# An attention and gated-MLP kernel: tokens by batches of 576 instead of chunks of 512, and each weight piece loaded once

## The chip, the cores and the metric

One Trainium2 chip, one of its cores. The metric is device time in microseconds (us), the median of several executions. Beside them one execution was taken by the hardware profiler; all durations below come from that one.

## The reference

Two stages on the same tokens. Attention has 8 batches, 8 heads, 576 positions and 64 columns a head; its output is the sum of a coarse attention over means of four positions, repeated four times, and a local attention in which a position sees those less than four away. The 4608 tokens of 512 columns then go through a gated MLP whose three weights come as float64:

```python
def _moe_ref(x, w_gate, w_val, w_out):          # x 4608x512, gate and val 512x1536, out 1536x512
    gate = 1.0 / (1.0 + np.exp(-(x @ w_gate)))
    val = x @ w_val
    return (gate * val @ w_out).astype(np.float32)

def _attn_ref(q, k, v):                         # each 8x8x576x64
    ...
    out_up = np.repeat(out_d, factor, axis=2)   # attention on means of 4 positions
    ...
    out_local = np.matmul(attn, v)              # mask: abs(i - j) < 4
    return (out_up + out_local).astype(np.float32)
```

## The kernel before, in words

**Attention units.** Two heads of one batch make a unit, four units a batch, 32 in all (`unit_steps`). A unit sums four positions on GpSimd (`prep2`, `vdsum`), forms the local scores (`s`) and the coarse ones (`sd`) on TensorE, normalizes both on VectorE, ScalarE and GpSimd, transposes them (`at`, `adt`), multiplies with v (`x`, `od`), adds the two (`xs`), and writes 576 columns of the MLP's input `xT` as two float16 tiles, a high part and a low part. Units 0 to 7 (the first two batches) multiply in float32, later ones in float16 parts.

**Weights.** Each weight is 12 pieces of 128x512 float64 words, 512 KB each: `wg`, `wv` and `wo`, 36 pieces. All 36 are loaded twice. In the first pass (`wstep` with "m") VectorE takes the largest magnitude of a piece from its high words (`wmax`, L153, tile `hmx`). When the `wg` and `wv` pieces of a group (0 to 3, 4 to 11), or all of `wo`, have theirs, a maximum over all partitions gives their scale (`wscale`, `gscales`, `ratios`). In the second pass (`wstep` with "c", `wconv`) a piece is loaded again; ScalarE multiplies its high words by the scale `hc` (L206), VectorE makes a float32 of the two words by a shift (L207), an or (L208) and the merging of the sign bit (L209), and the float32 is split into two float16 parts: by ScalarE (L215) and GpSimd (L216) for `wg` and `wv`, by ScalarE (L157) and VectorE (L158) for `wo`.

**MLP.** Tokens go in nine chunks of 512, and the weights in twelve steps `fc` a chunk: `moe_gate` (12 matmuls of 512 columns into `pg`, then tanh on ScalarE, L622, in one to two segments, as a chunk can lie in two batches), `moe_val` (12 matmuls into `pv`; VectorE multiplies, L630; ScalarE and VectorE split the product into float16, L638 and L639), `moe_out` (12 matmuls, three into each of the four output banks `po`). A product of float16 pairs is three matmuls (`product`, L395). The four `po` banks stay open for a whole chunk, so `wo`'s pieces are wanted one by one.

**PSUM.** Six banks belong to the MLP (`pg`, `pv`, four `po`), two to attention (`ps_a`).

**Order.** A table `T` gives each step a position, `add` collects the steps, and they are issued in the order of their positions; a scheduler then orders the instructions of each engine. Up to position `c1` = 56 the first two batches of attention, the weights and chunk 0 are woven together; from there each step of three matmul blocks (gate, val, out of the step before) takes the attention steps due. `awake` fills TensorE's waits of the first batch with matmuls on zeros. All loads and stores go through SyncE's queue (SP), in order.

Of the kernel before, what the change touches and what calls it, by code (L numbers as in the profile page):

```python
# [9 lines left out]
F16 = mybir.dt.float16  # L10
# [9 lines left out]
T = dict(ma=4.5, mas=0.45, mb=9.5, mbs=0.5, c1=56, gs=2.66, g0=16.84, r1=1.99, rs=1.6, ob=3.16, v0=15.13, v1=16.62, v2=17.5, vs=2.12, o0=18, os=1.2, pro=2.36, u4=13.82, u5=21, u6=27, u7=32, l4=1.3, l5=2.77, l6=9.47, l7=8.68, lv=15.08, vm=1.58, b8=6.75, s8=6.63, b12=26.05, s12=8.17, hold=32.07, al=0.76, am=1, z=3.68, sd=0, sn=0.79, v0m=0.61, xd=[2, 3, 7], ad=[0, 3, 7], aa=[0, 1, 2, 3, 6], td=[0, 3, 9, 10], vd=[], a_prep1=-2.43, a_prep2=-0.89, a_s0=0.01, a_s1=0.52, a_sm=1.82, a_d0=2.39, a_d1=2.6, a_dn=5.17, a_a0=4.37, a_vd=2.6, a_a1=5.1, a_v=2.74, a_at=5.22, a_od=5.79, a_x=8.38, m_prep0=-3.14, m_prep1=-1.14, m_prep2=-1.43, m_s0=0.69, m_s1=2.59, m_sm=3.12, m_d0=2.84, m_d1=5.8, m_a0=10, m_dn=10.78, m_vd=11.67, m_a1=12, m_v=13.07, m_at=13.44, m_od=15.64, m_x=17, k0=30, k_prep1=4, k_prep2=0, k_s0=2, k_s1=2, k_sm=4, k_d0=3, k_d1=0, k_dn=0, k_a0=3, k_vd=8, k_a1=2, k_v=5, k_at=0, k_od=0, k_x=0)  # L20
# [6 lines left out]
R = 58  # L27
# [8 lines left out]
NCHUNK = NT // CH  # L36
NFC = DFF // P
# [7 lines left out]
NWT = 1 + 2 * NPC  # L45
NST = 5
# [3 lines left out]
WAHEAD = 1  # L50
MAHEAD = 3
WGROUPS = [(0, 4), (4, NPC)]
SIGNBIT = -(1 << 31)


# [3 lines left out]
def attention_moe(ctx, tc, qk, qkd, v, vd, wg, wv, wo, mask, out):  # L59
# [5 lines left out]
    ps_o = ctx.enter_context(tc.tile_pool(name="ps_o", bufs=1, space=PSUM))  # L65
    ps_a = ctx.enter_context(tc.tile_pool(name="ps_a", bufs=2, space=PSUM))

# [3 lines left out]
    def awake(n):  # L73
        pt = ps_o.tile([P, 512], F32, tag="val", name="awake")
        for i in range(n):
            nc.tensor.matmul(pt[:, :256], idle[:, :P], idle, start=True, stop=True)

    awake(T["k0"])
# [4 lines left out]
    wg16 = cp.tile([P, NFC, 2, 4, P], F16, tag="wg16", name="wg16")  # L83
    wv16 = cp.tile([P, NFC, 2, 4, P], F16, tag="wv16", name="wv16")
    wo16 = cp.tile([P, NFC, 2, DM], F16, tag="wo16", name="wo16")
# [7 lines left out]
    def borrow(i, n):  # L93
        taken[i] += n
        return room[i][:, NFC * WPC - taken[i] : NFC * WPC - taken[i] + n]

    def zeroed(eng, shape, dtype, name):
# [59 lines left out]

# [698 lines left out]
```

## Time and profile before

| | |
|---|---|
| runs | 1107.99, 1111.20, 1111.18 us; median 1111.18 |
| the profiled execution | 1110.07 us, of which the span from first to last instruction is 1108.3 us |
| mean granted TensorE clock | 0.973 |
| busy over the span | TensorE 96%, VectorE 49%, ScalarE 40%, GpSimd 33% |
| moved | 99.84 MB read, 9.44 MB written |

PE is TensorE, PEld its weight loads, DVE VectorE, ACT ScalarE, POOL GpSimd, SP SyncE. A busy TensorE is one that has a matmul in flight, which tells nothing of useful work: the fillers count, and a matmul at the lower clock counts longer. The profile's page also follows the chain of work that ended last, and lists groups of instructions with their mean time and with the idle time in front of them.

### The profile page before, as it was taken

The numbers are of one execution on the slowest core, as the hardware profiler recorded it, in microseconds if no ns is written. First come the engines' busy times: TensorE is split into PE (matmuls) and PEld (weight loads), VectorE is DVE, ScalarE is ACT, GpSimd is POOL, SyncE is SP. The second block draws the span as 40 slices with busy tenths as digits, with TensorE's granted clock in tenths as the row PEclk, the third lists the DMA queues.
The fourth block names the chain that finished last, engine by engine and source line by source line (L and its number), as shares of the span: only waits on it lengthen the run. The fifth ranks groups of instructions, "written<-read, shape, count | busy, mean of one in ns | idle before, by whom it ended". The sixth has DMA issues, their size and how long they took to land.

```text
span 1108.3 us, 17149 instructions
## 1 busy us (share of the span) xinstructions
PE 1062.2 (96%) x6831; PEld 554.8 (50%) x6831; DVE 547.4 (49%) x1038; ACT 444.1 (40%) x1048; POOL 364.6 (33%) x426
## 2 busy tenths in 40 slices
PE   8768878999998999999999999999999999999998
PEld 6543434655554555555555555555555544444443
DVE  5779989763445444444444444444444422212112
ACT  5535656443444443444334443444344422112112
POOL 8535755332433443333333443333332200000000
PEclk9859988999999999999999999999999999999999
DMA  9987866331213222232212221321120000000001
GB/s 361 382 313 262 275 211 210 110 118 59 70 56 136 70 71 70 71 109 71 70 57 101 74 80 59 109 71 59 59 97 1 2 1 38 1 1 38 1 1 38
DMA packets 31903, 110.38 MB, mean 100 GB/s; under 512 B 3536, under 2 KB 3664, under 8 KB 31824
## 3 DMA queue, kind: packets, MB, share of 16 engines
q1 hardware_dynamic: 31824, 109.30, 29.0%
q8 instruction: 54, 0.88, 0.3%
q14 instruction: 25, 0.20, 0.1%
HBM read 99.84 MB, written 9.44 MB: 99 GB/s over the span
## 4 chain that ended last, share of the span: by engine, by line
PE 86%; DVE 7%; POOL 2%; DMA 2%; ACT 2%; issue 1%; SPq 0%; DVEq 0%; POOLq 0%
PE po L395 25%; PE pv L395 24%; PE pg L395 23%; PE s L395 3%; PE x L395 3%; PE sd L395 3%; PE od L395 2%; PE at L543 2%; PE adt L553 1%; DMA qkd<-in_qkd_dram 1%; DVE hmx L153 1%; DVE wrv L209 1%; DVE wrg L208 1%; POOL kdblk L386 1%; DMA wg6c<-in_wg_dram 0%
## 5 line engine op out<-in xcount | busy, mean ns | idle before, releaser
L395 PE MATMUL pg<-xT,wg 128*128 128x512 f16 x1296 | 312.5, 383 | 11.2 <-ACT wg L215 7.3
L395 PE MATMUL pv<-xT,wv 128*128 128x512 f16 x1296 | 310.3, 381 | 5.3 <-DVE tanh L630 3.1
L395 PE MATMUL po<-g,wo 128*128 128x512 f16 x1188 | 281.2, 379 | 0.0
L395 PEld LDWEIGHTS <-wg 128*128 128x128 f16 x1296 | 125.3, 98 | 158.3 <-ACT wg L215 8.6
L395 PEld LDWEIGHTS <-wo 128*128 128x128 f16 x1296 | 126.4, 98 | 150.8 <-ACT wo L157 3.9
L395 PEld LDWEIGHTS <-wv 128*128 128x128 f16 x1296 | 125.6, 98 | 150.1 <-issue 6.4
L630 DVE SCALAR_TENSOR_TENSOR tanh<-tanh,pv 128x512 f32<-128x512 f32 x108 | 73.9, 684 | 210.2 <-PE pv L395 206.4
L622 ACT ACTIVATE tanh<-pg,tsc 128x512 f32<-128x512 f32 (+7 forms) x192 | 86.7, 497 | 176.4 <-PE pg L395 176.2
L638 ACT ACTIVATE g<-tanh,gs 128x512 f16<-128x512 f32 x99 | 71.4, 721 | 137.4 <-DVE tanh L630 135.6
L639 DVE SCALAR_TENSOR_TENSOR g<-tanh,gs,g 128x512 f16<-128x512 f32 x99 | 84.1, 849 | 52.9 <-ACT g L638 52.5
L477 POOL TENSOR_TENSOR t<-t,mx 128x640 f32<-128x640 f32 x32 | 43.4, 1357 | 164.0 <-DVE mx L476 160.1
L596 POOL TENSOR_TENSOR xT<-xs,xT 128x384 f16<-128x384 f32 (+7 forms) x54 | 48.5, 911 | 48.1 <-ACT xT L594 47.5
L585 DVE TENSOR_TENSOR xs<-x,od 128x464 f32<-128x464 f32 (+1 forms) x56 | 23.5, 452 | 72.3 <-PE x L395 72.3
L487 POOL TENSOR_TENSOR t<-t,sm 128x640 f32<-128x640 f32 x28 | 36.1, 1290 | 68.9 <-DVE sm L485 61.3
L465 DVE SCALAR_TENSOR_TENSOR t<-s,mk 128x384 f32<-128x384 f32 x64 | 30.8, 485 | 54.8 <-PE s L395 54.7
L157 ACT ACTIVATE vblk<-v,svb 64x640 f16<-64x640 f32 x48 | 39.6, 825 | 34.3 <-PE x L395 33.6
L395 PEld LDWEIGHTS s<-qk 64*64 64x64 f32 x1200 | 41.0, 138 | 21.5 <-issue 16.3
L158 DVE SCALAR_TENSOR_TENSOR vblk<-v,svb,vblk 64x640 f16<-64x640 f32 x48 | 47.9, 998 | 3.8 <-ACT vblk L157 1.7
L395 PE MATMUL s<-qk 64*64 64x64 f32 x1200 | 48.9, 227 | 0.6 <-ACT adt L535 0.6
L528 POOL TENSOR_TENSOR ad<-e,sme 72x288 f32<-72x288 f32 x52 | 37.1, 733 | 35.2 <-DVE sme L519 34.8
L511 ACT ACTIVATE e<-sd,mxd 72x144 f32<-72x144 f32 x128 | 47.1, 371 | 2.8
L384 POOL TENSOR_TENSOR qkd<-qkd 128x576 f32<-128x576 f32 x29 | 35.0, 1208 | 37.6 <-DMA qkd<-in_qkd_dram 36.9
(295 smaller groups left out, 1105.1 us busy)
## 6 DMA issues: line engine op xcount, KB each, us to landing
qk<-in_qk_dram SPq DMA_DIRECT2D x30, 610.0 KB, 3.9
qkd<-in_qkd_dram SPq DMA_DIRECT2D x29, 576.0 KB, 3.7
vd<-in_vd_dram SPq DMA_DIRECT2D x29, 384.0 KB, 3.1
v<-in_v_dram SPq DMA_DIRECT2D x32, 320.0 KB, 3.0
out_dram<-osb SPq DMA_DIRECT2D x16, 512.0 KB, 2.6
wo<-in_qk_dram SPq DMA_DIRECT2D x2, 610.0 KB, 9.9
wo<-in_qkd_dram SPq DMA_DIRECT2D x2, 576.0 KB, 9.5
out_dram<-osb SPq DMA_DIRECT2D x4, 256.0 KB, 2.4
```

The costliest lines, as they stand in the source:

```text
L157: nc.scalar.activation(hi, src, AF.Copy, scale=sc)
L158: nc.vector.scalar_tensor_tensor(out=lo, in0=src, scalar=sc, in1=hi, op0=ALU.mult, op1=ALU.subtract)
L395: nc.tensor.matmul(o, w[a], x[c], start=first and i == 0, stop=last and i == len(pairs) - 1)
L477: nc.gpsimd.tensor_tensor(out=t, in0=t, in1=mx.unsqueeze(2).to_broadcast([P, NBLK, WIN]), op=ALU.subtract)
L487: eng.tensor_tensor(out=t, in0=t, in1=sm.unsqueeze(2).to_broadcast([P, NBLK, WIN]), op=ALU.mult)
L511: nc.scalar.activation(s["e"][:, qb, h, :], pt[:QM, h * SD : (h + 1) * SD], AF.Exp, bias=mx[:, h : h + 1], scale=QKSCALE / 16, accum_out=s ...
L528: eng.tensor_tensor(out=AD[:, qb].rearrange("p c h k -> p h c k")[:, :, :, :KC], in0=s["e"][:, qb].rearrange("p h (c k) -> p h c k", c=NKC ...
L596: eng.tensor_tensor(out=x[:, hp, 1, o : o + n], in0=src, in1=x[:, hp, 0, o : o + n], op=ALU.subtract)
L622: nc.scalar.activation(t[:, o : o + n], pt[:, o : o + n], AF.Tanh, scale=tsc[:, b, fc : fc + 1])
L630: nc.vector.scalar_tensor_tensor(out=t, in0=t, scalar=1.0, in1=pt, op0=ALU.add, op1=ALU.mult)
L638: nc.scalar.activation(g[:, 0], t, AF.Copy, scale=gs[:, fc : fc + 1])
L639: nc.vector.scalar_tensor_tensor(out=g[:, 1], in0=t, scalar=gs[:, fc : fc + 1], in1=g[:, 0], op0=ALU.mult, op1=ALU.subtract)
```

## The change

- The MLP takes one batch of 576 tokens at a time, in two halves of 288 columns. A gate or val step is 24 matmuls of 288 columns in one PSUM tile of two banks (`mm`, two such tiles); tanh and the product take 576 columns in one instruction.
- `moe_out` does not run beside the gate and val steps any more. The float16 products of all twelve steps of a batch are kept (`gq`), and then four output blocks of 72 matmuls each run over all twelve `wo` pieces.
- Attention has four PSUM banks in place of two.
- A weight piece is loaded once. ScalarE multiplies its high words by a constant, VectorE makes the float32 at once (shift, or, sign) into the float16 home of the next piece, and its magnitude is taken from that float32 (`wjoin`). The scale comes later, for two pieces of `wg` and `wv` at a time (`wscale`), and is put on in `wsplit`: for `wg` and `wv` by one more VectorE instruction, for `wo` within the split. `wo` is scaled when all twelve magnitudes are known (`oscale`).
- Staging buffers are four in place of five, v buffers four in place of five; loads stand in one fixed order (`load`).
- The table `T` is new: it gives every step of the first four units its own position.

```diff
+HN = S // 2
-NST = 5
+NST = 4
-WGROUPS = [(0, 4), (4, NPC)]
+WGROUPS = [(0, 2), (2, 4), (4, 6), (6, 8), (8, 10), (10, NPC)]
-    ps_o = ctx.enter_context(tc.tile_pool(name="ps_o", bufs=1, space=PSUM))
-    ps_a = ctx.enter_context(tc.tile_pool(name="ps_a", bufs=2, space=PSUM))
+    ps_m = ctx.enter_context(tc.tile_pool(name="ps_m", bufs=2, space=PSUM))
+    ps_a = ctx.enter_context(tc.tile_pool(name="ps_a", bufs=4, space=PSUM))
+    def mm(name):
+        return ps_m.tile([P, 2, 512], F32, tag="mm", name=name)
...
-    def wmax(t, o):
-        absmax(o, t[:, :, 1].bitcast(F32))
...
-    def wconv(k, i, t, j):
+    def wjoin(k, i, after):
+        t = wraw.pop((k, i))
         h, l = t[:, :, 1], t[:, :, 0]
-        a = raw.tile([P, WPC], I32, tag="wa", name=f"wr{k}{i}", bufs=3)
-        nc.scalar.activation(h.bitcast(F32), h.bitcast(F32), AF.Copy, scale=hc[:, j : j + 1])
-        nc.vector.tensor_scalar(out=a, in0=h, scalar1=3, scalar2=None, op0=ALU.logical_shift_left)
+        a = wwide(k, i).bitcast(I32)
+        nc.scalar.activation(h.bitcast(F32), h.bitcast(F32), AF.Copy, scale=WORDS)
+        with behind(after):
+            nc.vector.tensor_scalar(out=a, in0=h, scalar1=3, scalar2=None, op0=ALU.logical_shift_left)
         nc.vector.scalar_tensor_tensor(out=a, in0=l, scalar=29, in1=a, op0=ALU.logical_shift_right, op1=ALU.bitwise_or)
         nc.vector.scalar_tensor_tensor(out=a, in0=h, scalar=SIGNBIT, in1=a, op0=ALU.bitwise_and, op1=ALU.bitwise_or)
+        absmax(hmx[:, j : j + 1], wwide(k, i))
...
+    def wsplit(k, i):
+        a = wwide(k, i)
+        hi, lo = (home[k][:, wslot(k, i), e] for e in range(2))
         if k == "o":
-            split(wo16[:, i, 0, :], wo16[:, i, 1, :], a.bitcast(F32), co[:, i : i + 1])
+            split(hi, lo, a, sc)
         else:
-            nc.scalar.copy(hi, src)
-            nc.gpsimd.tensor_tensor(out=lo, in0=src, in1=hi, op=ALU.subtract)
+            nc.vector.tensor_scalar(out=a, in0=a, scalar1=sc, scalar2=None, op0=ALU.mult)
+            nc.scalar.copy(hi, a)
+            nc.gpsimd.tensor_tensor(out=lo, in0=a, in1=hi, op=ALU.subtract)
...
+    def moe_in(b, w, x, k, fc, name):
+        pt = mm(name)
+        for h in range(2):
+            f = slice(h * HN, (h + 1) * HN)
+            for j in reversed(range(4)):
+                product(pt[:, h, :HN], [w[:, fc, a, j, :] for a in range(2)], [x[:, j, e, f] for e in range(2)], j == 3, j == 0)
+        return pt[:, :, :HN]
...
-    def moe_out(c, fc):
-        for e in range(4):
-            product(oacc[c][e], [wo16[:, fc, a, f] for a in range(2)], [g[:, a] for a in range(2)], fc == 0, fc == NFC - 1)
+    def moe_out(b, m):
+        assert all(("o", i) in done for i in range(NPC))
+        pt = mm(f"po_{b}_{m}")
+        for h in range(2):
+            for n in range(NFC):
+                fc = n // 2 + NFC // 2 * (n % 2)
+                product(pt[:, h, :HN], [wo16[:, wslot("o", fc), a, m * P : (m + 1) * P] for a in range(2)],
+                        [gq[:, fc, e, h * HN : (h + 1) * HN] for e in range(2)], n == 0, n == NFC - 1)
```

Where the instructions stand now, first on VectorE at the first weights of batch 0. Before, two conversions of the second pass (here `wg` and `wv` of step 8; `...c` is a piece loaded for conversion, `...m` one loaded for its maximum, `tanh` an MLP product):

```order
L207 TENSOR_SCALAR wrg_1362<-wg8c 128x512
L209 SCALAR_TENSOR_TENSOR wrv_1312<-wv7c,wrv_1312 128x512
L207 TENSOR_SCALAR wrv_1403<-wv8c 128x512
L208 SCALAR_TENSOR_TENSOR wrg_1362<-wg8c,wrg_1362 128x512
L153 TENSOR_REDUCE hmx<-wo11m 128x1
L630 SCALAR_TENSOR_TENSOR tanh_6_1564<-tanh_6_1564,pv_6_1595 128x512
L208 SCALAR_TENSOR_TENSOR wrv_1403<-wv8c,wrv_1403 128x512
L209 SCALAR_TENSOR_TENSOR wrg_1362<-wg8c,wrg_1362 128x512
```

And now, at the scaling of steps 2 and 3 and the first MLP product (L209 to L211 are the shift, the or and the sign, L160 the magnitude, L251 the scaling; `wg_109` and `wv_110` are the float16 homes):

```order
L160 TENSOR_REDUCE hmx<-wg_109 128x1
L160 TENSOR_REDUCE hmx<-wv_110 128x1
L251 TENSOR_SCALAR wg_109<-wg_109,cw 128x512
L251 TENSOR_SCALAR wv_110<-wv_110,cw 128x512
L251 TENSOR_SCALAR wg_109<-wg_109,cw 128x512
L251 TENSOR_SCALAR wv_110<-wv_110,cw 128x512
L209 TENSOR_SCALAR wg_109<-wg_927 128x512
L210 SCALAR_TENSOR_TENSOR wg_109<-wg_927,wg_109 128x512
L593 SCALAR_TENSOR_TENSOR tanh_0_852<-tanh_0_852,pv_0_876 128x576
```

The magnitude of a piece has stayed on VectorE and follows its own conversion; four scalings per two steps have come on top, in VectorE's queue ahead of the products.

Second, VectorE at the end of the weights. Before, the last three splits of `wo` (L158), with the MLP product of step 10 ahead of them and that of step 11 behind:

```order
L158 SCALAR_TENSOR_TENSOR wo_111<-wro_2062,co,wo_111 128x512
L583 SCALAR_TENSOR_TENSOR xs_2015<-x_8_2017,sxb,od_6_1959 128x112
L630 SCALAR_TENSOR_TENSOR tanh_10_1999<-tanh_10_1999,pv_10_2031 128x512
L209 SCALAR_TENSOR_TENSOR wro_2157<-wo11c,wro_2157 128x512
L639 SCALAR_TENSOR_TENSOR g_10_2045<-tanh_10_1999,gs,g_10_2045 128x512
L153 TENSOR_REDUCE vm_3148<-v_2991 128x1
L158 SCALAR_TENSOR_TENSOR wo_111<-wro_2111,co,wo_111 128x512
L158 SCALAR_TENSOR_TENSOR wo_111<-wro_2157,co,wo_111 128x512
L630 SCALAR_TENSOR_TENSOR tanh_11_2107<-tanh_11_2107,pv_11_2120 128x512
L639 SCALAR_TENSOR_TENSOR g_11_2134<-tanh_11_2107,gs,g_11_2134 128x512
```

And now, the last splits of `wo` (L165), between the attention of units 5 to 7 (`t`, `sm`, `xs`, `mxd`):

```order
L165 SCALAR_TENSOR_TENSOR wo_111<-wo_111,co 128x512 x2
L450 TENSOR_REDUCE sm_2281<-t_2160 128x10
L165 SCALAR_TENSOR_TENSOR wo_111<-wo_111,co 128x512
L550 SCALAR_TENSOR_TENSOR xs_2311<-x_0_2302,sxb,od_5_2279 128x464
L451 TENSOR_SCALAR sm_2281<-sm_2281 128x10
L165 SCALAR_TENSOR_TENSOR wo_111<-wo_111,co 128x512
L452 RECIPROCAL sm_2281<-sm_2281 128x10
L550 SCALAR_TENSOR_TENSOR xs_2311<-x_8_2313,sxb,od_5_2279 128x112
L165 SCALAR_TENSOR_TENSOR wo_111<-wo_111,co 128x512
L475 TENSOR_REDUCE mxd_1_2324<-sd_1_2322 72x2
```

All twelve splits of `wo` now come after the twelfth product of the first token block, where before they were spread among the products; 358 VectorE instructions stood up to the last split, and 382 stand there now.

Third, TensorE at the end of the first batch's output. `po_0` to `po_3` are the output blocks of the first 576 tokens, `x`, `od`, `adt`, `s` and `sd` attention of units 6 to 8, and `pg` and `pv` the next batch's first steps. Now:

```order
L367 MATMUL od_2593<-adt_7_2558,vdblk_117 128x144 x3
L367 MATMUL x_0_2601<-at_7_2435,vblk 128x58 x8
L367 MATMUL x_8_2612<-at_7_2435,vblk 128x58 x2
L367 LDWEIGHTS wo_111
L367 MATMUL po_3_2619<-gq,wo_111 128x288
```

Before, `wo` products of the first chunk began right behind the gate and val steps that fed them:

```order
L395 MATMUL s_3_1640<-qk_1143 64x64 x8
L395 MATMUL sd_0_1654<-kdblk_120,qks_1410 72x288
L395 LDWEIGHTS wo_111
L395 MATMUL po_0_1570<-wo_111 128x512
L395 LDWEIGHTS wo_111
L395 MATMUL po_0_1570<-wo_111 128x512
```

In the change the first two output blocks run side by side from behind unit 4's `x`, 35 matmuls of each ahead of the place where the last `wo` piece is wanted; behind it stand 37 of each, then 72 and 72 of the last two blocks.

## Rows read from the trace of the kernel before

**Rows 1.** The page's slices: the span in 40 slices of 27.7 us, busy tenths of TensorE and VectorE.

```profile
PE   8768878999998999999999999999999999999998
...
DVE  5779989763445444444444444444444422212112
```

**Rows 2.** Busy time by stretches of the span, first to second us: the length, then for each engine busy us and number of instructions, the granted clock (1.00 is 2.4 GHz, the lower level 0.50), DMA share, GB/s.

```profile
0.00:9.00 9.00, 7.87 (x77) 5.70 (x78) 2.31 (x6) 0.36 (x1) 5.44 (x12) 1.00 0.79 261
9.00:18.00 9.00, 6.65 (x69) 4.07 (x69) 7.66 (x16) 7.50 (x20) 8.54 (x13) 1.00 1.02 411
18.00:28.00 10.00, 9.91 (x93) 7.97 (x92) 6.57 (x16) 6.42 (x21) 8.49 (x13) 0.83 1.03 409
28.00:84.00 56.00, 39.89 (x241) 27.40 (x239) 44.39 (x100) 26.28 (x71) 22.26 (x28) 0.70 0.93 346
84.00:214.00 130.00, 111.62 (x627) 56.87 (x628) 123.85 (x224) 77.30 (x155) 74.40 (x62) 0.92 0.66 223
...
364.00:900.00 536.00, 536.00 (x3760) 282.45 (x3758) 247.28 (x475) 222.38 (x553) 193.27 (x237) 1.00 0.21 67
```

**Rows 3.** VectorE in order of time around 214 us: start us, duration us, engine, line, operation, out<-in, shapes, count, and in brackets the idle time before it with what ended it.

```profile
206.32 0.68 DVE L209 SCALAR_TENSOR_TENSOR wro<-wo10c,wro 128x512 int32<-128x512 int32 x1
...
212.60 1.40 DVE L158 SCALAR_TENSOR_TENSOR wo<-wro,co,wo 128x512 f16<-128x512 f32 x2
216.07 0.69 DVE L630 SCALAR_TENSOR_TENSOR tanh<-tanh,pv 128x512 f32<-128x512 f32 x1 [2.08 <-PE pv L395]
```

**Rows 4.** TensorE in order of time at the end of the span (columns as in rows 3); a row is a run of instructions of one kind.

```profile
1090.62 2.75 PE L395 MATMUL po<-g,wo 128*128 128x512 f16 x12
1093.20 2.75 PE L395 MATMUL pg<-xT,wg 128*128 128x512 f16 x12
1095.80 2.75 PE L395 MATMUL pv<-xT,wv 128*128 128x512 f16 x12
1098.38 5.34 PE L395 MATMUL po<-g,wo 128*128 128x512 f16 x24
```

**Rows 5.** TensorE from 640 to 672 us (columns as in rows 3): the run of short matmuls and the row behind it.

```profile
650.35 0.98 PE L395 MATMUL x<-at,vblk 128*128 128x58 f16 x30
651.17 0.81 PE L395 MATMUL po<-g,wo 128*128 128x512 f16 x3
```

**Rows 6.** Groups of TensorE instructions from 364 to 900 us: line, engine, operation, out<-in, shapes, count, busy us, mean ns of one, idle us before.

```profile
L395 PE MATMUL pg<-xT,wg 128*128 128x512 f16 x675 | 162.5, 379 | 0.0
L395 PE MATMUL pv<-xT,wv 128*128 128x512 f16 x672 | 161.6, 379 | 0.0
L395 PE MATMUL po<-g,wo 128*128 128x512 f16 x672 | 161.1, 379 | 0.0
L395 PE MATMUL s<-qk 64*64 64x64 f32 x720 | 28.7, 223 | 0.0
...
L395 PE MATMUL x<-at,vblk 128*128 128x58 f16 x600 | 20.0, 189 | 0.0
```

**Rows 7.** Groups of VectorE instructions over the span, shapes apart (columns as in rows 6, with the releasers of the idle time).

```profile
L639 DVE SCALAR_TENSOR_TENSOR g<-tanh,gs,g 128x512 f16<-128x512 f32 x99 | 84.1, 849 | 52.9 <-ACT g L638 52.5
L630 DVE SCALAR_TENSOR_TENSOR tanh<-tanh,pv 128x512 f32<-128x512 f32 x108 | 73.9, 684 | 210.2 <-PE pv L395 206.4 <-ACT t L478 1.9 <-ACT e L511 1.1
...
L508 DVE TENSOR_REDUCE mxd<-sd 72x2 f32<-72x288 f32 x64 | 28.6, 446 | 33.5 <-PE sd L395 33.4
...
L153 DVE TENSOR_REDUCE vm<-v 128x1 f32<-128x640 f32 x32 | 26.0, 815 | 35.4 <-DMA v<-in_v_dram 35.3
...
L518 DVE TENSOR_SCALAR sme<-sme 72x4 f32<-72x4 f32 x32 | 9.1, 285 | 20.7 <-ACT e L511 20.6
...
L487 DVE TENSOR_TENSOR t<-t,sm 128x640 f32<-128x640 f32 x4 | 3.6, 904 | 0.1
L158 DVE SCALAR_TENSOR_TENSOR xT<-xs,sxb,xT 128x512 f16<-128x512 f32 x4 | 3.4, 861 | 0.3 <-ACT xT L157 0.3
L583 DVE SCALAR_TENSOR_TENSOR xs<-x,sxb,od 128x464 f32<-128x464 f32 x4 | 2.8, 692 | 2.6 <-PE x L395 2.6
...
L158 DVE SCALAR_TENSOR_TENSOR xT<-xs,sxb,xT 128x64 f16<-128x64 f32 x4 | 1.4, 338 | 0.0
L583 DVE SCALAR_TENSOR_TENSOR xs<-x,sxb,od 128x112 f32<-128x112 f32 x4 | 1.3, 324 | 0.0
```

**Rows 8.** The conversion's three VectorE operations by stretch (L207 the shift, L208 the or, L209 the sign, in this order; of L207 both stretches): stretch, its length, VectorE busy us and count, clock, DMA share, GB/s.

```profile
18.00:84.00 66.00, 1.68 (x4) 0.72 0.95 356
84.00:214.00 130.00, 16.90 (x32) 0.92 0.66 223
...
84.00:214.00 130.00, 26.16 (x33) 0.92 0.66 223
...
84.00:214.00 130.00, 29.12 (x33) 0.92 0.66 223
```

**Rows 9.** VectorE from 126 to 140 us (columns as in rows 3): the sign merging of a `wg` piece.

```profile
133.21 1.46 DVE L209 SCALAR_TENSOR_TENSOR wrg<-wg7c,wrg 128x512 int32<-128x512 int32 x1
```

**Rows 10.** GpSimd in the same stretch.

```profile
132.97 1.15 POOL L216 TENSOR_TENSOR wv<-wrv,wv 128x512 f16<-128x512 f32 x1
```

**Rows 11.** Waits over the span: engine and line, what was waited for, us in total, times, the longest.

```profile
DVE tanh L630 <- PE pv L395: 206.4, 70, 5.5
...
DVE vm L153 <- DMA v<-in_v_dram: 35.3, 18, 5.6
```

## What the change does to the time, predicted

> **What bounds the kernel now.** I read the slices first, then the busy time by stretches, then the order of time on VectorE and TensorE at the border between them. The slices [rows 1] show two kernels in one: to about 210 us VectorE is at 7 to 9 tenths, from there TensorE stands at 9 to the end. The stretches [rows 2] sharpen it. From 84 to 214 us VectorE is busy 123.85 of 130 us; from 364 to 900 us TensorE is busy 536.00 of 536.00 and VectorE 247 of it. Before 28 us the DMA engines are full (share 1.02, 1.03), to 84 us nearly (0.93). The border is the last `wo` split [rows 3]: two splits end at 214.0 us, and the next product already waits 2.08 us for TensorE. So the span is **the time at which VectorE has finished the weights, plus TensorE's work that stands behind it**. Behind it come 1108.3 - 214.0 = 894.3 us. The last matmul ends at 1098.38 + 5.34 = 1103.7 us [rows 4], so 4.6 us of that are the last output's way out.
>
> Of the first 214 us VectorE is busy 2.31 + 7.66 + 6.57 + 44.39 + 123.85 = 184.8 and idle 29.2: 8.0 to 18 us, 15.0 from 18 to 84 us, 6.2 after [rows 2].
>
> **The change on VectorE.** The orders give 358 instructions up to the last split before and 382 now; by kind:
>
> - Shift, or, sign and the magnitude stay at 36 each: the second load goes, its VectorE work does not, for a magnitude was the first pass's only work there. Nothing.
> - 24 scalings of `wg` and `wv` (L251) are new: float32, 512 columns, in place. The nearest row is the shift, one input and a scalar: 16.90/32 = 0.53 us, and 1.68/4 = 0.42 in the quieter stretch [rows 8]. The other side is an instruction of 512 float32 columns with two inputs, one in PSUM, 0.684 [rows 7]. 24 x 0.53 = +12.7 (10.1 to 16.4), since the stretch is the crowded one.
> - MLP products: 12 pairs of 576 columns now stand before the last split, where 11 of 512 stood. A pair is 0.684 + 0.849 = 1.53 us [rows 7]; 12 x 1.53 x 1.125 - 11 x 1.53 = 20.7 - 16.9 = +3.8.
> - Two more normalizing products `t` at 0.904: +1.8. Five v magnitudes fewer at 0.815: -4.1. Part of unit 7 falls behind (`xs` 0.692 + 0.324, one `mxd` 0.446, one `sme` and its reciprocal, together some 0.45): -1.9. Four `xT` low parts in one piece of 576, between 0.861 and 0.861 + 0.338 each, say 0.97: -0.9 [all rows 7]. The small instructions on scales even out by count (some 45 against 47).
> - Crowding: in 84 to 214 us an or takes 26.16/33 = 0.79 and a sign merging 29.12/33 = 0.88 [rows 8], while an undisturbed one takes 0.68 [rows 3]; one of 1.46 us [rows 9] runs beside a GpSimd subtraction of 1.15 us [rows 10]. Now the joining comes earlier than the splits. If a third of the 33 x (0.11 + 0.20) = 10 us goes, that is -3 (0 to -10).
>
> Busy: 184.8 + 12.7 + 3.8 + 1.8 - 4.1 - 1.9 - 0.9 - 3 = 193.
>
> Idle: the 8.0 us at the start are the first unit's and stay; the 6.2 late ones I keep. The 15.0 from 18 to 84 us I put down mostly to loads: v magnitudes alone wait 35.3 us for them over the span [rows 11], and that stretch has the full DMA. Now 18.9 MB less come in and a loaded piece gives VectorE 2.4 us of work at once instead of a 0.67 us magnitude, so I keep 3 (0 to 15). Total idle 17. **The last split ends at 193 + 17 = 210 us**, 4 us earlier than now. The halved weight loading is thus worth little: it ran beside a VectorE that has as much to do.
>
> **The change on TensorE.** A matmul of 512 columns takes (1098.38 - 1090.62)/36 = 0.2156 us [rows 4]. One of 288 isn't in the trace in float16. Between (651.17 - 650.35)/30 = 0.0273 for 58 columns [rows 5] and 0.2156 for 512, a straight line gives 0.1227; pro rata without any fixed part it would be 0.1213. I take 0.1227: a weight load that took longer than 58 columns would show in that row. The MLP has 8 x 864 = 6912 matmuls now against 3888: 848 us against 838, +10, although the columns are the same.
>
> What can't start before the last `wo` piece is the point. Before, `wo` products ran as their pieces came, and 214 us found ten steps of the first chunk out. Now 35 matmuls of each of the first two output blocks stand ahead of the last piece, and 37 + 37 + 72 + 72 = 218 behind it: 218 x 0.1227 = 26.7 us. Then
>
> - what is left of units 6 and 7 in float32: some 7 us;
> - seven batches: 7 x 864 x 0.1227 = 742;
> - 24 units of attention. From 364 to 900 us 2019 MLP matmuls [rows 6] at 0.2156 take 435.3 of 536 us, and 100.7 remain; 600 `x` matmuls at 30 a unit are 20 units, 720 `s` at 40 are 18 (a few records are missing), 19.3 by what stands in that stretch, so 5.2 us a unit: 125 (120 to 134);
> - waits in the batches: +2. The gate and val tiles are two, so one must be emptied while the other fills. That was 2 x 2.59 us, now 24 x 0.1227 = 2.94, while product and tanh grow by an eighth;
> - the tail, 4.6.
>
> Together 907 us. **Span 210 + 907 = 1117, and with the 1.8 us that the profiled execution has around its span 1119 us**, against its own 1110.07 (the median of the runs shown, 1111.18, lies 1.1 above it). The 4 us of earlier weights are outweighed by 13 us more on TensorE: 218 + 6048 = 6266 matmuls take 769 us, where before (894.3 - 4.6 - 7 - 125)/0.2156 = some 3515 of 512 columns were left for 758; these are nearly the same columns (6266 x 288/512 = 3525), so +9 of it is the fixed part of a matmul, paid nearly twice as often.
>
> What is hidden: the float16 products kept for a batch, the four attention banks, tanh in one instruction and the new load order. From 227 us on TensorE covers all these; if it had idle time there, VectorE's 247 of 536 us still leave room.
>
> **Rivals.**
>
> 1. *Forecast* (0.44): VectorE keeps the border near 210 us, output stands behind.
> 2. *The joining gets much cheaper and the loads free VectorE* (0.29, ends faster). Against my 0.53 + 0.79 + 0.88 = 2.20 us for the three conversion steps stand the undisturbed 0.42 + 0.68 + 0.68 = 1.78 [rows 3, 8]. With splits later, half the pieces or more may be joined undisturbed, and the scalings too: 36 x 0.42 = 15 us and 24 x 0.11 = 2.6, of which -3 is already in; with idle time at 11, the early 8 and 3 more, the border is at about 191 us and the end near 1100. It decides from about 200 us down: there the gain covers the 13 us that TensorE gets on top. For it speaks the DMA share in the early stretch; against it that from 84 us VectorE is 95% busy with the DMA at 0.66, where loads can't be what it waits for.
> 3. *It cancels* (0.16): the border at 200 to 206 us, the end within 1108 to 1114.
> 4. *Two tiles for gate and val are too few* (0.10, slower). VectorE's product waits for TensorE 70 times now, up to 5.5 us [rows 11]: slack that the shorter block halves. If one in four of the 168 blocks of the last seven batches waits 0.6 us, that is +25: 1143.
> 5. *The weight loads come out from behind the matmuls* (0.01). From 364 to 900 us a load is 282.45/3758 = 0.075 us [rows 2], and 3024 more of them in the open would give +227: 1346. The row of 58 columns, a load and a matmul in 0.027 us, excludes it nearly.
>
> The Trainium skill, TensorE: Matmul & The Clock Gate, section Part 3, The mechanism, says that a weight load overlaps matmuls in flight only when the row groups differ; all these use the full array, and by that rule the fifth case would be the forecast. The trace disagrees: 36 pairs in 7.76 us leave 2.3 ns a pair beyond 512 columns at 2.4 GHz.
>
> **How the numbers follow.** About 0.3% (3.3 us) is what a measurement of this kernel can tell from no change, 1107.8 to 1114.5 us. Slower is the forecast, the fourth and fifth case, 0.55; same the third, 0.16; faster the second, 0.29. The forecast alone runs from 1112 (scalings at 0.42, crowding gone by half) to 1132 (0.684, no relief, six more us of idle). The range reaches down into the second case and up to the weaker half of the fourth: 1095 to 1140.
>
> **What the changed profile would show.** Right: the last `wo` split near 210 us with VectorE at 90% or more from 60 us on; 24 scalings of some 0.5 us; the first batch's output as a dense run on TensorE right behind, 27 us of matmuls; blocks of 24 in 2.94 us; no idle TensorE from 250 us; a lower DMA share before 84 us. Wrong: a last split below 200 us (second case), VectorE with long waits for DMA or scales before 150 us, TensorE waiting for `tanh` or `gq` in later batches (fourth), or a granted clock that falls while TensorE waits for `wo`, which would stretch the output at the lower level.

## The result, and the profile after

The changed kernel takes 1118.95 us (median of 5 runs, 1117.19 to 1122.24), the kernel before 1111.18. The ratio is 1.0078, 95% interval 1.0055 to 1.0101: slower by 0.8%. The forecast was 1119. The sum came out right; the event that it took for the border (the end of the last `wo` split) did not stand, and two of its terms were off by 3 and 5 us in opposite directions. The profiled execution took 1117.19 us, its span is 1115.4.

Busy tenths by slice, and busy time by the stretches of [rows 1, 2], now of the changed kernel:

```profile
PE   9695688999999999999999999999999999999998
...
DVE  7969999735552446314452346315452345302210
```

```profile
0.00:9.00 9.00, 7.95 (x73) 5.78 (x74) 2.79 (x7) 0.83 (x1) 6.93 (x15) 1.00 0.81 300
9.00:18.00 9.00, 9.00 (x100) 7.36 (x101) 7.30 (x21) 6.15 (x18) 7.05 (x12) 1.00 1.03 411
18.00:28.00 10.00, 9.93 (x114) 8.50 (x112) 9.83 (x17) 6.13 (x21) 8.04 (x10) 1.00 1.03 408
28.00:84.00 56.00, 44.06 (x298) 35.52 (x298) 45.80 (x99) 32.36 (x77) 19.48 (x17) 0.73 0.27 88
84.00:214.00 130.00, 99.19 (x835) 73.80 (x833) 126.20 (x244) 63.60 (x134) 62.77 (x56) 0.89 0.48 163
364.00:900.00 536.00, 536.00 (x5222) 430.97 (x5221) 231.54 (x446) 181.40 (x413) 171.09 (x204) 1.00 0.22 73
```

From 84 to 214 us VectorE is busy 126.20 of 130 us, as forecast, and TensorE less than before (99.19 against 111.62). From 28 to 84 us the DMA share has fallen from 0.93 to 0.27, yet VectorE idles 10.2 us there, against 11.6 before. From 18 to 84 us, the stretch of the prediction, it idles 10.4 us against 15.0.

TensorE in order of time, where the first batch's output begins and where the last `wo` split is wanted (in brackets the idle time and what ended it):

```profile
185.70 0.27 PE L135 MATMUL mxt<-ident,m1o 128*1 128x128 f32 x1 [2.79 <-DVE m1o L229]
...
194.80 2.58 PE L367 MATMUL po<-gq,wo 128*128 128x288 f16 x10 [1.78 <-ACT wo L164]
...
213.24 9.24 PE L367 MATMUL po<-gq,wo 128*128 128x288 f16 x74 [0.40 <-DVE wo L165]
222.32 0.90 PE L367 MATMUL od<-adt,vdblk 128*128 128x144 f32 x6
```

The last split ends at 213.2 us, and 74 output matmuls follow at (222.32 - 213.24)/74 = 0.1227 us each, the value taken in the prediction. But TensorE waits only 0.40 us there. Its last long waits are those at 185.7 us, for the maximum over the twelve magnitudes of `wo` (`m1o`), and at 194.8 us, for the first split. From there on output and attention fill it. The ten matmuls at 194.8 us took 2.58 us, where ten at 0.1227 take 1.23: the granted clock was 0.57 from 194 to 198 us, mostly the lower level of 1.2 GHz, behind the wait of 1.78 us. The prediction had named this as a sign of being wrong; it cost some 1.4 us.

The same view of the kernel before shows that there too the border was earlier than the prediction had it:

```profile
145.47 0.27 PE L126 MATMUL mxt<-ident,m1o 128*1 128x128 f32 x1
...
178.71 0.87 PE L395 MATMUL po<-wo 128*128 128x512 f16 x2 [2.83 <-ACT wo L157]
180.70 4.45 PE L395 MATMUL po<-wo 128*128 128x512 f16 x10 [1.12 <-DVE wo L158]
```

From 180.7 us on TensorE is without a wait until 345 us, though VectorE converts until 214: it had output products in hand. The first row is the maximum over the magnitudes of `wo`: it stood at 145.5 us, where it now stands at 185.7.

### The profile page after: what moved, and what is told of

Read it like the earlier page. It is cut to its first block, busy times and chain, and to the rows that moved or that the text cites. A ratio compares the mean times of both kernels' runs of the same rounds, so it can differ in the third digit from the quotient of the medians.

```text
span 1115.4 us, 23080 instructions
## 1 busy us (share of the span) xinstructions
PE 1067.4 (96%) x9935; PEld 853.8 (77%) x9935; DVE 544.6 (49%) x1046; ACT 393.6 (35%) x878; POOL 345.9 (31%) x395
## 4 chain that ended last, share of the span: by engine, by line
PE 84%; DVE 9%; ACT 2%; DMA 2%; POOL 1%; issue 1%; DVEq 0%; ACTq 0%; SPq 0%; POOLq 0%
PE po L367 25%; PE pg L367 22%; PE pv L367 22%; PE s L367 3%; PE x L367 3%; PE sd L367 2%; PE od L367 2%; PE at L510 1%; DVE hmx L160 1%; PE awake L83 1%; PE adt L520 1%; DMA wg<-in_wg_dram 1%; DVE wg L211 1%; DMA wo<-in_wo_dram 1%; DVE wv L210 1%
## 5 line engine op out<-in xcount | busy, mean ns | idle before, releaser
L367 PE MATMUL pg<-xT,wg 128*128 128x288 f16 x2304 | 307.2, 290 | 15.9 <-ACT wg L252 15.3
L367 PE MATMUL pv<-xT,wv 128*128 128x288 f16 x2304 | 302.0, 286 | 3.7 <-DVE tanh L593 3.5
L367 PE MATMUL po<-gq,wo 128*128 128x288 f16 x2304 | 289.9, 287 | 2.2 <-ACT wo L164 1.8
L367 PEld LDWEIGHTS <-wg 128*128 128x128 f16 x2304 | 225.2, 99 | 79.7 <-ACT wg L252 15.9
L367 PEld LDWEIGHTS <-wv 128*128 128x128 f16 x2304 | 224.2, 98 | 60.8 <-issue 4.1
L367 PEld LDWEIGHTS <-wo 128*128 128x128 f16 x2304 | 224.0, 98 | 59.9 <-ACT wo L164 2.1
L593 DVE SCALAR_TENSOR_TENSOR tanh<-tanh,pv 128x576 f32<-128x576 f32 x96 | 72.1, 751 | 200.4 <-PE pv L367 200.4
L164 ACT ACTIVATE gq<-tanh 128x576 f16<-128x576 f32 x96 | 65.6, 683 | 198.1 <-DVE tanh L593 197.4
L588 ACT ACTIVATE tanh<-pg,tsc 128x576 f32<-128x576 f32 x96 | 70.8, 738 | 125.6 <-PE pg L367 125.4
L165 DVE SCALAR_TENSOR_TENSOR gq<-tanh,gq 128x576 f16<-128x576 f32 x96 | 77.8, 810 | 23.8 <-ACT gq L164 22.9
L165 DVE SCALAR_TENSOR_TENSOR vblk<-v,svb,vblk 64x640 f16<-64x640 f32 x48 | 46.6, 971 | 5.1 <-ACT vblk L164 4.3
```

Source lines behind the costliest of these rows:

```text
L164: nc.scalar.activation(hi, src, AF.Copy, scale=sc)
L165: return nc.vector.scalar_tensor_tensor(out=lo, in0=src, scalar=sc, in1=hi, op0=ALU.mult, op1=ALU.subtract)
L367: nc.tensor.matmul(o, w[a], x[c], start=first and i == 0, stop=last and i == len(pairs) - 1)
L588: nc.scalar.activation(t, pt, AF.Tanh, scale=tsc[:, b, fc : fc + 1])
L593: nc.vector.scalar_tensor_tensor(out=t, in0=t, scalar=1.0, in1=pt, op0=ALU.add, op1=ALU.mult)
```

## The experiments

All edits are to the changed kernel, but for the fourth run. "Last join" below is the end of the magnitude of the last `wo` piece, the last VectorE step ahead of the scale of `wo`.

**1. Scaling on ScalarE.**

```diff
-            nc.vector.tensor_scalar(out=a, in0=a, scalar1=sc, scalar2=None, op0=ALU.mult)
+            nc.scalar.activation(a, a, AF.Copy, scale=sc)
```

> The changed kernel, with the 24 scalings of the gate and val weights put on by ScalarE in place of VectorE; nothing is left out. Theory (VectorE's work up to the last wo split sets the border, and TensorE's work behind it is fixed): 24 instructions that took 11.9 us in the changed kernel leave VectorE, the last split ends near 201 us instead of 213.2, and the time is 1107 us (1105 to 1110). Rival (the weights come through a chain in which ScalarE or the loads are late, and VectorE only looks full because it is given its work late): ScalarE gets 24 x 0.63 = 15 us ahead of the splits, the border stays at 211 to 215 and the time at 1117 to 1121.

1112.23 us, ratio to the kernel before 1.0009 (0.9997 to 1.0022): 6.7 us of the 12, between the ranges of the two. VectorE's busy time up to the last join fell by 11.0 us, its idle time grew by 4.2 (waits for `x` and for tanh), the join came 6.9 us earlier and the span ended 5.1 us earlier. The theory holds in kind; what VectorE is given back is spent in part on other waits.

**2. More fillers on TensorE.**

```diff
-    known = {}
+    known = {}; [add(p, lambda n=n: awake(n)) for p, n in ((29.2, 70), (35.9, 10), (36.9, 10), (38.0, 10))]
```

> The changed kernel, with 100 filler matmuls on zeros more on TensorE where it waits for VectorE between 39 and 68 us. Theory (VectorE's idle 10.4 us between 18 and 84 us are waits for the x products of units 2 and 3, which run at the lower clock because TensorE had stood idle 8.5 us before): the two runs of 20 x matmuls take 2.3 us in place of 4.1 and 4.2, VectorE's waits of 1.98 and 4.25 us shrink, the border comes 3 to 5 us earlier, 1114 us (1112 to 1117). Rival (these waits are loads, as the prediction had it for the kernel before, or other chains that take the place): the border stays within 1 us, 1118 to 1120.

1125.97 us, 1.0127 (1.0104 to 1.0149): slower by 7, as neither theory said. The fillers came in front of unit 1's `od` and of what follows, the first gate matmul moved from 68.8 to 75.0 us, and the clock fell again all the same in the waits for ScalarE behind them (`x` at 60 and 69 us took 4.36 us a run). Nothing on VectorE's waits follows from this run.

**3. Each piece loaded twice into its buffer.**

```diff
         load(t.rearrange("p a b -> p (a b)"), srcs[k][i].bitcast(I32))
+        load(t.rearrange("p a b -> p (a b)"), srcs[k][i].bitcast(I32))
```

> The changed kernel, with every weight piece loaded twice into the same buffer, the second load behind the first: 18.9 MB more, as many bytes of weights as before the change. Theory (the loads run beside a VectorE that has as much to do): 0 to +3 us, 1118 to 1122, with VectorE still over 95% busy from 84 us. Rival (the single load is worth much, and other costs of the change have eaten it): +8 us or more, 1127 and up, with VectorE waiting for weights before 150 us.

1156.87 us, 1.0406 (1.0383 to 1.0429): the rival's side. The second load waits for the end of the first: SyncE's queue waits 36 times for the landing of a weight piece, 157 us in all, and what stands behind waits with it. VectorE's longest waits from 18 to 244 us are then those of its shift (L209) for ScalarE's multiplying (L207) of a late piece:

```profile
DVE wg L209 <- ACT wg L207: 12.7, 6, 4.0
DVE wv L209 <- ACT wv L207: 11.8, 9, 3.0
DVE wo L209 <- ACT wo L207: 6.8, 7, 1.9
```

This prices a wait in the load queue, not the bytes; run 8 parts the two.

**4. The kernel before, with gate and val matmuls in halves of 256.**

```diff
-        for k in range(4):
-            product(pt, [wg16[:, fc, a, k, :] for a in range(2)], [x[:, k, e, :] for e in range(2)], k == 0, k == 3)
+        for h in range(2):
+            hs = slice(h * CH // 2, (h + 1) * CH // 2)
+            for k in range(4):
+                product(pt[:, hs], [wg16[:, fc, a, k, :] for a in range(2)], [x[:, k, e, hs] for e in range(2)], k == 0, k == 3)
```

The val matmuls are cut in the same way.

> The kernel before, with each gate and val matmul of 512 columns cut into two of 256, each with its own weight load: 2592 matmuls and loads more, same columns. Theory (a matmul has a fixed part of some 2.3 ns and its load is hidden): 2592 x 2.3 ns = +6.0 us, of which 5.4 stand behind the border: the ratio to the kernel before is 1.005 (1.003 to 1.007), 1116 to 1117 us. Rival (a load can't run beside a matmul that uses the same rows of the array): 2592 x 0.075 = +194 us. Second rival (shorter matmuls cost nothing, and the changed kernel's later end comes from elsewhere): within 1 us of the kernel before.

1110.05 us, 0.9987 (0.9968 to 1.0006): by its time the second rival. The trace tells more. TensorE at the end of the span:

```profile
1085.93 2.78 PE L395 MATMUL pg<-xT,wg 128*128 128x256 f16 x24
1088.55 2.78 PE L395 MATMUL pv<-xT,wv 128*128 128x256 f16 x24
1091.17 2.75 PE L395 MATMUL po<-g,wo 128*128 128x512 f16 x12
1093.76 2.78 PE L395 MATMUL pg<-xT,wg 128*128 128x256 f16 x24
```

24 halves take 2.62 us, 12 whole ones 2.59: 0.1092 and 0.2158 us, a fixed part of 2.5 ns each beyond the columns at 2.4 GHz. From the first output's scaling to TensorE's end the kernel before needs 879.0 us less 3.5 idle, this one 883.2 less 2.1: +5.6, near the 5.4 expected. But its first output was scaled 3.6 us earlier (221.1 against 224.7 us), as the first chunk's steps stand in another order (the first `wo` product at 156.1 us, before at 160.6), and that hid it. The load beside the matmul costs nothing, as forecast.

The Trainium skill (TensorE: Matmul & The Clock Gate, Part 3, The mechanism) lists a load as overlapping matmuls in flight only where the row groups differ; this trace disagrees: 24 full-array loads and matmuls took 2.62 us.

**5. The instruction of 3.87 us in two.** On VectorE at the scale of `wo` one instruction on 12 columns stands out, and right behind it the first split:

```profile
190.11 3.87 DVE L236 TENSOR_SCALAR co<-ew,rv,so 128x12 f32<-128x12 f32 x1
...
194.77 1.69 DVE L165 SCALAR_TENSOR_TENSOR wo<-wo,co 128x512 f16<-128x512 f32 x2
```

```diff
-        nc.vector.tensor_scalar(out=co, in0=ew[:, :, 1], scalar1=rv, scalar2=so, op0=ALU.mult, op1=ALU.mult)
+        nc.vector.tensor_scalar(out=co, in0=ew[:, :, 1], scalar1=rv, scalar2=None, op0=ALU.mult)
+        nc.vector.tensor_scalar(out=co, in0=co, scalar1=so, scalar2=None, op0=ALU.mult)
```

> The changed kernel, with the one instruction that works out the twelve wo scales (two scalars from memory, 12 columns, 3.87 us at 190.1 us) written as two instructions of one such scalar each; nothing is left out. Theory (the handover to TensorE is the first wo split: TensorE's last long waits in the changed kernel end at 194.8 us with it, and the 916 us of work behind are fixed): two instructions of 0.2 us, the first split 3 to 3.6 us earlier, 1115.5 us (1114.5 to 1117). Theory of the prediction (handover at the last split): the same, as VectorE as a whole gets 3.5 us free. Rival (the 3.87 us are a wait for something else): same time, 1118 to 1120.

1118.54 us, 1.0064 (1.0048 to 1.0081): the rival. The first of the two took 0.23 us, elsewhere; the second, in the old place, this:

```profile
190.22 3.51 DVE L236 TENSOR_SCALAR co<-co,so 128x12 f32<-128x12 f32 x1
193.76 0.21 DVE L238 TENSOR_SCALAR so<-eo,ev 128x1 f32<-128x1 f32 x1
```

GpSimd in the same microseconds of this run:

```profile
189.31 1.28 POOL L495 TENSOR_TENSOR ad<-e,sme 72x288 f32<-72x288 f32 x2 [2.32 <-DVE sme L486]
190.55 1.25 POOL L444 TENSOR_TENSOR t<-t,mx 128x640 f32<-128x640 f32 x1
191.77 1.14 POOL L356 TENSOR_TENSOR qkd<-qkd 128x576 f32<-128x576 f32 x1
192.87 0.82 POOL L356 TENSOR_TENSOR vd<-vd 128x384 f32<-128x384 f32 x1
193.66 0.93 POOL L358 TENSOR_TENSOR kdblk<-qkd 64x144 f32<-64x144 f32 x2
```

The VectorE instruction ends at 193.73 us, as the GpSimd instruction on `vd` does (193.69), while GpSimd goes on with the next. In runs 6, 7 and 8 GpSimd stands otherwise, and the unsplit instruction takes 0.32, 0.28 and 0.28 us. The first split comes no sooner for it: it ends 10.7 to 11.9 us behind the last join in those three runs, 10.1 us in the changed kernel. So no run shows that the 3.87 us make the change slower.

**6. The low parts of ten `wo` pieces left to GpSimd as zeros.**

```diff
-        if k == "o":
+        if k == "o" and i in (0, NPC // 2):
             split(hi, lo, a, sc)
+        elif k == "o":
+            nc.scalar.activation(hi, a, AF.Copy, scale=sc)
+            nc.gpsimd.memset(lo, 0.0)
```

> The changed kernel, with the low part of ten of the twelve wo pieces set to zero by GpSimd in place of VectorE's ten subtractions (10 x 0.87 us, all behind the first two splits); this leaves out part of the computation. Theory of the prediction (the last wo split sets the border at 213.2 us): the border comes 7 to 9 us earlier and so does the end, 1110 to 1112 us. Theory from TensorE's waits (the first wo split at 194.8 us sets it; behind it TensorE waits only 0.4 us more in the changed kernel, since attention and the output blocks fill it): 0 to -1.5 us, 1117.5 to 1119.

1117.99 us, 1.0056 (1.0040 to 1.0072): 1 us, as by the second theory, not 7 to 9. Its last VectorE split ends at 198.8 us instead of 213.2, and VectorE is busy 18.25 us from 185 to 214 us in place of 27.45:

```profile
185.00:214.00 29.00, 26.75 (x241) 22.43 (x242) 18.25 (x45) 20.88 (x53) 19.20 (x30) 0.82 0.27 92
```

The span did not end earlier (1117.1 against 1115.4). Part of that is TensorE's clock, granted 0.82 in this stretch against 0.94 in the changed kernel: 29 x 0.12 = 3.5 us of full speed, so the time alone does not decide. TensorE's waits do. Behind 185.7 us the changed kernel has 1.78 + 0.40 us of them, and this run has one of 0.40 us, for ScalarE: no more than some 2 us could be gained here. The prediction's border falls: VectorE's work behind the first splits is not on the path.

**7. Pieces 4 and 5 not held.** `-B1=4` `+B1=6` in the table: their joining no longer waits for unit 3's `xT`.

> The changed kernel, with the joining of weight pieces 4 and 5 (gate and val) no longer held back behind unit 3's MLP input. Theory (the 10.4 us that VectorE idles from 18 to 84 us in the changed kernel are the held joins: 6.2 us of it are waits for the x products of units 2 and 3 with no other work given): the two waits of 1.98 and 4.25 us are filled by two of the joins of 2.4 us, VectorE's idle time up to the last split falls by 3 to 5 us and the end comes 2 to 5 us earlier, 1114 to 1117. Rival (the joins push the attention of unit 3 back by as much): within 1.5 us, 1117.5 to 1120.5. Rival (loads): VectorE waits for ScalarE's scaling of a late piece instead, no gain.

1117.44 us, 1.0056 (1.0036 to 1.0075): at the edge of the first rival's 1117.5 to 1120.5. The first gate matmul moved from 68.8 to 73.9 us, idle time from 18 to 84 us stayed (10.3), the last join came at 186.7 us against 185.4. VectorE's waits for ScalarE's multiplying of a loaded piece, the second rival's, are 2.6 us in this stretch against 1.4.

**8. 18.9 MB more, beside.**

```diff
         load(t.rearrange("p a b -> p (a b)"), srcs[k][i].bitcast(I32))
+        load(junk[NPC * "gvo".index(k) + i], srcs[k][i].bitcast(I32))
```

`junk` is a scratch area in device memory, one place for each piece.

> The changed kernel, with 18.9 MB more moved: behind the load of each weight piece stands a second transfer of the same piece to a scratch area in device memory, which nobody waits for but the next load. Unlike the run with both loads into one buffer, no piece is held up by its own second load. Theory (weight bytes beside a VectorE that has as much to do cost little): 0 to +4 us, 1118 to 1123. Rival (the loads as such set the early stage, and the change gained by halving them): +15 us or more, 1134 and up, with VectorE's idle time before 213 us grown by as much.

1111.12 us, 1.0005 (0.9995 to 1.0014): faster than the changed kernel by 8 us, as neither said, with as many weight bytes read as before the change. Its stretches from 28 to 84 and 84 to 150 us:

```profile
28.00:84.00 56.00, 47.30 (x321) 38.04 (x321) 50.70 (x106) 32.77 (x79) 22.11 (x20) 0.76 0.68 258
84.00:150.00 66.00, 44.94 (x332) 31.49 (x330) 63.61 (x123) 27.24 (x44) 19.40 (x15) 0.82 0.89 334
```

More bytes (share 0.68 and 0.89), and VectorE idles 5.3 us in the first stretch, not 10.2 (2.4 in the second, where the changed kernel idles 1.0). So the bytes do not make VectorE's waits before 84 us, and whatever they cost is less than what this run gained. The order of the early instructions is another one here, which is taken for the cause without a test of its own: unit 3's input is done earlier, the first gate matmul stands at 64.5 us, the last join at 178.4.

**9. Pieces 2 and 3 held.**

```diff
-        JBEHIND.append(("g", 0, max(i - T["BO"], 0)) if k == "o" else None if i < T["B1"] else ("x", 3) if i < T["B2"] else ("g", 0, max(i - T["B3"], 0)))
+        JBEHIND.append(("g", 0, max(i - T["BO"], 0)) if k == "o" else None if i < 2 else ("x", 1) if i < T["B1"] else ("x", 3) if i < T["B2"] else ("g", 0, max(i - T["B3"], 0)))
```

> The changed kernel, with the joining of weight pieces 2 and 3 (gate and val) held back behind the MLP input of unit 1, so that VectorE normalizes units 2 and 3 earlier; nothing is left out. It copies, without the extra bytes, what stood otherwise in the run with 18.9 MB more, where the first gate matmul came at 64.5 us in place of 68.8 and the last wo join ended at 178.4 us in place of 185.4. Theory (the end is the last wo join, reached by VectorE's busy and idle time up to it, and some 926 us behind; the order of attention and joins before 60 us makes its idle time): first gate matmul at 65 to 67 us, the last join at 180 to 183 us, 1113 to 1117 us. Rival (the extra bytes themselves, or chance, made that run faster): 1118 to 1120.

1123.18 us, 1.0108 (1.0093 to 1.0123): slower by 4, which neither said. Unit 2's input came 0.4 us earlier, unit 3's did not, and VectorE waited 7.19 us for its `x` in one piece; the first gate matmul stood at 69.5 us. What made run 8 fast is not copied by this, and which part of its order it was stays open.

**10. Runs 1 and 9 together.**

> The kernel with held pieces 2 and 3 and, with it, the 24 scalings of gate and val weights on ScalarE; nothing is left out. Theory (VectorE's busy and idle time up to the last wo join add up): the gain of the scalings alone (6.7 us) and of the held pieces alone add, within 2 us: 1107 to 1111. Rival (both fill the same idle time): no more than the better of the two, 1112.

1112.37 us, 1.0011 (1.0001 to 1.0020): the rival; holding neither gains nor costs here.

**11. And the first batch's low parts on GpSimd.**

```diff
-        mark["g", b, fc] = split(*[gq[:, fc, e].rearrange("p (h c) -> p h c", h=2) for e in range(2)], t, GSC).ins
+        hi, lo = [gq[:, fc, e].rearrange("p (h c) -> p h c", h=2) for e in range(2)]
+        if b == 0:
+            nc.scalar.activation(t, t, AF.Copy, scale=GSC)
+            nc.scalar.copy(hi, t)
+            mark["g", b, fc] = nc.gpsimd.tensor_tensor(out=lo, in0=t, in1=hi, op=ALU.subtract).ins
+        else:
+            mark["g", b, fc] = split(hi, lo, t, GSC).ins
```

> As the kernel with held pieces and scalings on ScalarE, and the first batch's twelve low parts of the MLP product (12 x 0.78 = 9.3 us on VectorE) made by GpSimd behind one more ScalarE instruction each; nothing is left out. Theory (VectorE's time up to the last wo join): the last join comes 5 to 9 us earlier than without it and the end as much, 1101 to 1106. Rival (GpSimd's subtractions slow VectorE's instructions beside them, as the one that took 3.87 us beside four GpSimd instructions): what is taken away comes back in longer joins, 1108 to 1112.

1106.85 us, 0.9962 (0.9951 to 0.9974): below both kernels, 0.85 us above the theory's range and nearer to it than to the rival. The theory's "as much" did not hold: against run 10 the last join came 20.5 us earlier and the time fell by 5.5.

**12. Runs 1 and 11 without holding.**

> The changed kernel with the 24 scalings on ScalarE and the first batch's twelve low parts of the MLP product on GpSimd, but without the held pieces 2 and 3; nothing is left out. Theory (holding the two pieces gains nothing, as the run with it alone showed, and the gain of the kernel with all three comes from VectorE's work taken away): 1104 to 1108 us, the last wo join near 160 us, TensorE's wait for wo behind the twelfth step gone. Rival (the three only work together): 1109 to 1112.

1105.65 us, 0.9945 (0.9928 to 0.9961): the best, 0.55% below the kernel before. Its stretches:

```profile
84.00:150.00 66.00, 50.41 (x400) 36.77 (x399) 65.97 (x113) 43.56 (x74) 34.92 (x25) 0.95 0.63 205
150.00:185.00 35.00, 32.74 (x299) 24.52 (x297) 30.40 (x67) 21.87 (x49) 33.06 (x29) 0.95 0.29 108
```

VectorE is still full to 150 us, but idles 4.6 of 35 us then, where the changed kernel idles 1.3. The gain, 13 us, is less than the 18.7 us by which VectorE's work up to the last join fell: the next bound is near.

**The kernels together.** VectorE's busy and idle time up to the last join, and what of the span is left behind it (us, worked out from each trace):

| kernel | busy | idle | last join | span | behind |
|---|---|---|---|---|---|
| changed | 164.9 | 20.5 | 185.4 | 1115.4 | 930.0 |
| 1 scaling on ScalarE | 153.9 | 24.7 | 178.5 | 1110.3 | 931.8 |
| 2 fillers | 170.5 | 23.4 | 193.9 | 1124.0 | 930.1 |
| 3 loads twice | 164.4 | 52.6 | 216.9 | 1156.4 | 939.5 |
| 5 scale in two | 164.8 | 20.4 | 185.1 | 1117.2 | 932.1 |
| 6 no low parts | 166.1 | 20.5 | 186.6 | 1117.1 | 930.5 |
| 7 not held | 166.6 | 20.1 | 186.7 | 1118.0 | 931.3 |
| 8 bytes beside | 162.4 | 16.0 | 178.4 | 1109.2 | 930.8 |
| 9 held | 169.0 | 21.0 | 190.0 | 1120.4 | 930.4 |
| 10 = 1 + 9 | 152.4 | 26.6 | 179.0 | 1108.5 | 929.5 |
| 11 = 10 + GpSimd | 144.5 | 14.0 | 158.5 | 1104.4 | 945.9 |
| 12 = 1 + GpSimd | 146.2 | 18.6 | 164.8 | 1104.9 | 940.1 |

In nine of the twelve rows the part behind is 929.5 to 932.1 us, while the join moves over 15 us: the end follows the last `wo` join one for one. It follows the twelfth val step of the first batch nearly as well: in these rows that step ends 0.0 to 3.7 us ahead of the join, and 929.5 to 934.6 us of the span are left behind it. Runs 11 and 12 part the two. There the join is no longer last; the twelfth val step ends at 181.5 and 180.2 us, later than the join, the first output matmul follows it at 182.3 and 180.4 us, and only 922.9 and 924.7 us are left behind it. So the wait for the join and the scale is what stood between the val step and the output.

## Why the prediction was right, and where it was not

- *VectorE's busy time* up to the last split: 193 forecast, 191.1 measured. Groups of VectorE's instructions up to 215 us:

```profile
L211 DVE SCALAR_TENSOR_TENSOR wg<-wg,wg 128x512 int32<-128x512 int32 x12 | 11.9, 994 | 0.0
...
L165 DVE SCALAR_TENSOR_TENSOR gq<-tanh,gq 128x576 f16<-128x576 f32 x12 | 9.3, 777 | 0.5 <-POOL qks L358 0.4
...
L593 DVE SCALAR_TENSOR_TENSOR tanh<-tanh,pv 128x576 f32<-128x576 f32 x12 | 8.9, 743 | 0.0
...
L251 DVE TENSOR_SCALAR wv<-wv,cw 128x512 f32<-128x512 f32 x12 | 6.1, 511 | 0.0
...
L251 DVE TENSOR_SCALAR wg<-wg,cw 128x512 f32<-128x512 f32 x12 | 5.8, 480 | 0.0
```

  The scalings took 11.9 us (12.7 forecast), the MLP products 8.9 + 9.3 = 18.2 (20.7). The relief of crowding, -3, came to less than one: the durations of shift, or and sign of 36 pieces add up to 79.7 us now and 80.5 before. A sign of a `wg` piece still takes 0.99 us on average.
- *Idle time*: 17 forecast, 22.1 measured. The step "the 15.0 from 18 to 84 us I put down mostly to loads" failed. The wait row that it leaned on [rows 11] holds for the whole span. In this stretch of the kernel before, VectorE's waits for a load were 2.7 of the 15.0 us (0.7 more were for ScalarE's multiplying of a loaded piece), and the rest waits for ScalarE and TensorE:

```profile
DVE sme L518 <- ACT e L511: 3.3, 3, 1.5
...
DVE vm L153 <- DMA v<-in_v_dram: 1.3, 1, 1.3
DVE hmx L153 <- DMA wv8m<-in_wv_dram: 1.2, 1, 1.2
...
DVE hmx L153 <- DMA wg2m<-in_wg_dram: 0.2, 1, 0.2
```

  The changed kernel's waits in it are

```profile
DVE xs L552 <- PE x L367: 6.2, 2, 4.3
DVE wg L209 <- ACT wg L207: 1.4, 1, 1.4
```

  that is, mostly waits for unit 2's and 3's products on a TensorE at the lower clock (0.57 granted from 48 to 75 us): a run of 20 took 2.34 us at 37 us and 4.36 us at 63 us, behind 8.5 us without work. Of the 15.0 us 4.6 went, where the prediction had 12 go. Run 8 shows that the loads' bytes are not it.
- *The border*: 210 forecast, 213.2 measured for the last split. That it sets the end is wrong (run 6, and TensorE's 0.40 us of wait there). The lever is the last `wo` join with the scale behind it; the first split ends 10 us after it, and output and attention fill TensorE through the others. The sum held because it counted what TensorE had left behind the last split, 218 output matmuls and next to no wait, and that count is right whichever event set the moment.
- *The work behind the last split*: 907 forecast, 1115.4 - 213.2 = 902.2 measured. 218 output matmuls were 74 + 1 + 71 + 7 + 65 = 218; a block of 24 took 2.94 us; waits were 0 in place of 2, 24 units 121 in place of 125. This is 5 us less, the border 3 us more: the forecast's 1119 against the profiled 1117.19 owes that much to luck.
- *Why it is slower than before.* TensorE's last long wait for `wo` ended at 180.7 us before and ends at 194.8 now, since `wo` may not be scaled until all twelve magnitudes are in, and the output may not start until then. Of these 14 us some 6.5 come back: behind that wait TensorE ended after 923.0 us (3.5 of them idle) before and 916.5 now. Before, the first of the two loads gave the magnitudes, and their maximum went to TensorE at 145.5 us; with one load that is at 185.7. Halving the loads gave little to set against it: at most the 4.6 us of idle time on VectorE before 84 us. What delayed the last join is in good part the 24 scalings: with them off VectorE (run 1) 6.7 of the 7.8 us between the two medians are gone. The price of the later maximum by itself no run here shows.
- *The rivals.* The second rival's border adds up to 210 - 14.6 - 6 = 189 us by its own terms, not 191, and the low end of the forecast to 1114, not 1112; neither changes which case came. (36 pairs in 7.76 us leave 2.2 ns a pair, not 2.3.) Loads in the open did not come (run 4, and 536.00 of 536.00 us full at 0.1225 us a matmul). Two tiles for gate and val were enough: TensorE shows no wait behind the last split. Cheaper joining did not come. Runs 1 and 12 show that rival's lever nevertheless, with VectorE's work taken away by hand.

## What to carry to other kernels

Look for the last long wait of the engine that is full later, not for the last instruction of the engine that is full now: only work ahead of that wait is worth removing, and leaving out a later piece (run 6) shows it cheaply. Read a wait in its own stretch before a row of the whole span is put down to it. Where a scheduler places the instructions, an edit that should cost nothing can move the early stage enough to cost 4 us or gain 8 (runs 8 and 9): read the milestones in the trace (first gate matmul, last join) before believing a difference of that size.

## What the runs showed of the hardware that was not expected

A VectorE instruction of 12 columns took 3.87 us, and 3.51 as a half of it, beside back-to-back two-input GpSimd instructions, and ended within 0.04 us of the end of one of them, the one on `vd`; in runs 1, 2 and 10 it stood beside the same ones and took 3.87 or 3.88. In runs 6 to 9, 11 and 12 it took 0.28 to 0.32 us, though in 6 and 9 it stood beside a GpSimd instruction too. Splitting the instruction gained nothing. The rows show that it lasted until a GpSimd instruction ended; that GpSimd held it up, and by which resource, is argued from these times, for no run took the GpSimd instructions away alone.
